# Sixteen expert slots repacked into thirteen, and the rank product of every block one step later

## The chip, the cores and the metric

The kernel runs on one core of a Trainium2 chip. The metric is the device time of one execution in microseconds (us); of several runs the median counts. Engines are named as in the profile: PE is TensorE (its matmuls; PEld its loading of the stationary operand), DVE VectorE, ACT ScalarE, POOL GpSimd, SP SyncE.

## The reference

Three stages on 3072 tokens of 384 features (4 batches of 768, 8 heads of 48): a linear recurrence, a dense MLP with a leaky ReLU, and a layer of 8 experts of which each token uses the one with the highest score.

```python
for t in range(S):                                   # 768 steps
    cur = einsum('bhd,bhe->bhde', u * k[t], v[t])
    y[t] = einsum('bhd,bhde->bhe', r[t], state + cur)
    state = w[t][..., None] * state + einsum('bhd,bhe->bhde', k[t], v[t])
x = y.transpose(0, 2, 1, 3).reshape(3072, 384)
h = x @ w_in                                         # 384 -> 2048
x = (maximum(h, 0) + alpha * minimum(h, 0)) @ w_out  # 2048 -> 384
logits = normalized(x) @ normalized(expert_emb).T / tau
e = argmax(logits); gate = softmax(logits)[e]
out[e == i] = gate * (maximum(x[e == i] @ w1[i], 0) @ w2[i])   # 384 -> 1024 -> 384
```

With the reference's inputs the eight experts get 193, 578, 253, 951, 286, 327, 365 and 119 tokens.

## The kernel before

**Precision.** Every operand of a large product is split into a high part (fp32r) and the rest, and a product is three matmuls: high x high, high x low, low x high. Names that end in h and l are these parts.

**Stages.** The recurrence is computed in 24 tiles (n) of 128 tokens, in chunked form, while the MLP runs: MLP blocks j = 0 to 7 take three tiles (384 tokens) each, in 16 steps of 128 hidden features. In a step T, TensorE does nine matmuls of 384 columns for the first layer (L453) and nine of 392 for the second one of two steps earlier (L488; its 8 columns beyond 384 are the routing scores). Parts of the recurrence of later tiles stand between steps: transposes kt_ps (L341), a_ps (L352), u_ps (L368), y_ps (L391, L394) and t_ps (L409), which turns the result y (written by DVE at L400) into the input of the next block.

**Routing.** `route(j)` is a Python generator that is advanced once in every step. It computes for block j the one-hot matrix `oh` of the chosen experts on DVE (L550), yields as often as HOLD says (`HOLD[0]` for blocks 0 to 5, `HOLD[1]` and `HOLD[2]` for blocks 6 and 7), and then forms the rank product rk_ps on PE (L564 to L567): how many tokens ahead went to the same expert. DVE turns it into positions s_ps (L569, L570), and in the next step s_pf and s_pi (L573, L575). SP then writes the token rows (L580), and POOL scatters the token numbers to the table `tbl` by position (L583).

**PSUM.** rk_ps, kt_ps, the two a_ps, u_ps, t_ps and x_ps are tiles of one pool of three banks and take turns in them; the h tiles have two banks, the o tiles three.

**Expert slots.** After the MLP come the slots, whose kinds stand in the string KIND. A pair slot (P) takes 256 rows of one expert in eight steps, each with nine matmuls of 256 columns (l3, L796) and, two steps later, six of 384 (l4, L822). A single slot (S) takes 128 rows in two steps: nine matmuls of 512 columns each (l3_single, L832), four transposes (L843) and twelve matmuls of 384 (l4_single, L854). The first ES slots are early: a small table after block 6 gives each an expert that has 256 rows by then. The others come from the late table (`last_table`, after block 7), which DVE computes while the early slots run. `columns` finds for each late slot its expert and its first row, by comparing all slots with the running sums of slots per expert (`le`), and writes idsx (rows, L649, L652) and wix (weights, L655). What does not fit runs in an extra pass (`tile_extra`).

**Around a slot.** Its weights come in four loads (L754, POOL's indirect DMA), and eight pieces are split into high (ACT, L765) and low (DVE, L766) in the steps from four before the slot's first to three behind it. Its rows are gathered (L777) and transposed (x_T: PE L785, ACT L786, DVE L787). Between l3 and l4, ACT and DVE make the hidden values g2h (L800) and g2l (L801). At the end ACT scales each o by the gate (L859), and POOL scatters the rows to the output (L861).

Of the kernel before, what the change touches and what calls it, by code (L numbers as in the profile page):

```python
# [8 lines left out]
F32 = mybir.dt.float32  # L9
# [9 lines left out]
DM = H * D  # L19
# [26 lines left out]
ES = 5  # L46
NP = 6
NS1 = 5
NPX = 3
C_P = ES  # L50
C_S = ES + NP + NPX
NSLOT = C_S + NS1
KIND = "PPPPP" + "SPSPSPPSPSP"
COL = [s if s < ES else C_P + KIND[ES:s].count("P") if k == "P" else C_S + KIND[:s].count("S") for s, k in enumerate(KIND)]
# [6 lines left out]
HOLD = [1, 2, 2]  # L61
# [45 lines left out]
def tile_main(ctx, tc, keep, x2d, tbl, att, w_in, w_out, alpha, u_row, u_col, emb, tau, w1, w2, cst, out):  # L107
# [20 lines left out]
    u_sb = cp.tile([128, DM], F32, name="u_sb")  # L128
# [167 lines left out]
    def att_u(n):  # L296
        r_n, k_n = nat(n, 0), nat(n, 1)
        POOL.tensor_tensor(out=r_n, in0=r_n, in1=k_n, op=ALU.mult)
        POOL.tensor_tensor(out=r_n, in0=r_n, in1=u_sb, op=ALU.mult)
# [326 lines left out]
    def columns(c0, n, at, cu, step, base, odd):  # L626
# [5 lines left out]
        ei = once("ei", [128, NSLOT])[:, 0:m]  # L632
# [3 lines left out]
        jb = once("jb", [128, NSLOT])[:, 0:m]  # L636
# [12 lines left out]
        DVE.tensor_scalar(out=idsx[:, c0:c0 + n], in0=jb[:, 0:n], scalar1=prow, scalar2=None, op0=ALU.add)  # L649
        yield  # L650
        if m > n:
            DVE.tensor_scalar(out=idsx[:, c0 + n:c0 + m], in0=jb[:, n:m], scalar1=2.0, scalar2=prow, op0=ALU.mult, op1=ALU.add)  # L652
        DVE.tensor_scalar(out=ei, in0=ei, scalar1=float(NE - 1), scalar2=256.0, op0=ALU.min, op1=ALU.mult)
        for q in range(2):
            DVE.tensor_scalar(out=wix[:, q, c0:c0 + m], in0=ei, scalar1=prow2, scalar2=float(q), op0=ALU.add, op1=ALU.add)  # L655

    def early_table():

        yield WAIT
        tot = totals(NB - 2, oneb[:, 0:1])  # L660
        nb = above(tot, thr_full, "nb")
        cu = once("cu", [128, 2 * NE])[:, 0:NE]
# [3 lines left out]
        yield from columns(0, ES, at_early, cu, nb, None, None)  # L666
# [21 lines left out]
    def last_table():  # L688
# [42 lines left out]
        yield from columns(C_P, NP + NPX, at_last, cu, n, first[:, 0:1], o)  # L731
# [38 lines left out]
    def ids_load(s):  # L770
        t = sp.tile([128, 2], I32, tag="ids", name="ids", bufs=5)
        n = NTOK[s]
        POOL.indirect_dma_start(out=t[:, 0:n], out_offset=None, in_=tbl.rearrange("(n t) o -> n (t o)", t=n), in_offset=idx(idsx[:, COL[s]:COL[s] + 1]))
        ids_t[s] = t

    def gather(s, t):
        POOL.indirect_dma_start(out=xg[s % 3][:, t, :], out_offset=None, in_=x2d, in_offset=idx(ids_t[s][:, t:t + 1]), bounds_check=NT - 1, oob_is_err=False)  # L777

    def x_T(s, t):
        if t == 0:  # L780
            xT2[s] = [xp.tile([128, KD, SLOT], F32R, tag=f"x{i}", name=f"y{i}") for i in "hl"]
        hi, lo = (x[:, :, t * 128:(t + 1) * 128] for x in xT2[s])
        tp = ps_a.tile([128, KD, 128], F32, tag="a", name="x_ps")
        for k in range(KD):
            PE.transpose(tp[:, k, :], xg[s % 3][:, t, k * 128:(k + 1) * 128], ident)  # L785
        ACT.activation(out=hi, in_=tp, func=AF.Copy)  # L786
        DVE.tensor_tensor(out=lo, in0=tp, in1=hi.bitcast(F32), op=ALU.subtract)  # L787

    def l3(s, f):
# [8 lines left out]
        gh = gp.tile([128, SLOT], F32R, tag="gh", name="g2h")  # L798
        gl = gp.tile([128, SLOT], F32R, tag="gl", name="g2l")
# [68 lines left out]
    if True:  # L868
        for l in LOADS:
            if l == "e":  # L870
                SP.dma_start(out=en, in_=emb)
            elif l == "u":
                SP.dma_start(out=u_sb, in_=u_row.to_broadcast([128, DM]))
# [19 lines left out]
        POOL.memset(carry[0], 0.0)  # L893
        POOL.iota(ivals, pattern=[[0, BT], [1, NE]], base=0, channel_multiplier=0, allow_small_or_imprecise_dtypes=True)
# [187 lines left out]
        for s, k in enumerate(KIND):  # L1082
            U0, before = FIRST[s], KIND[s - 1]
            at(U0 + (9 if k == "P" else 3), o_scale, s)
            if k == "P":
# [11 lines left out]
            if s:  # L1097
                X = U0 - 4 if before == "P" else U0 - 2
# [248 lines left out]
def tile_kernel(ctx, tc, att, w_in, w_out, alpha, u_row, u_col, emb, tau, w1, w2, cst, r, k, v, w, uh, out):  # L1347
# [8 lines left out]
    wix = kp.tile([128, 2, NSLOT], I32, name="wix")  # L1356
# [68 lines left out]
```

## Time and profile before

| | |
|---|---|
| Median of three runs | 805.92 us (805.19 to 807.06) |
| Profiled execution | 808.39 us |
| Its span, first to last instruction | 806.6 us |
| Mean granted clock of TensorE | 0.994 |
| Busy: PE, DVE, ACT, POOL | 98%, 71%, 55%, 38% of the span |
| Moved by DMA | 114.85 MB, 142 GB/s over the span |

The profiled execution is one run of its own, and the rows below belong to it. A timeline row has the start and the duration of an instruction or of a group of alike ones, its engine and line, what it writes and reads, and, in brackets, how long the engine had been idle before it and what ended that. Matmuls overlap: the pitch from one start to the next is what each costs in a stream, and it is less than a duration.

### The profile page before, as it was taken

Reading aid. Unit: us, or ns where it says so; the run is one execution under the profiler, and the core shown is the slowest. Engines: PE = TensorE matmul, PEld = TensorE weight load, DVE = VectorE, ACT = ScalarE, POOL = GpSimd, SP = SyncE. Lnnn points to the kernel's source line nnn. Section 1 sums busy time; section 2 is a strip of 40 time slices with the busy share of each in tenths; the row PEclk is TensorE's granted clock in tenths of the full one; section 3 lists DMA queues with packets and bytes.
Section 4 is the critical chain, followed back from the end, with each engine's and each line's share of the span. In section 5 each row is a group of like instructions: output and inputs, shape, how many; then the busy total and the mean of one; then the engine's idle time right before and its main releaser. Section 6 shows DMA issues by size and latency. Waiting matters only on the chain. (4 is left out here: it accounts for less than half of the span.)

```text
span 806.6 us, 16527 instructions
## 1 busy us (share of the span) xinstructions
PE 791.2 (98%) x6507; PEld 755.1 (94%) x6507; DVE 570.7 (71%) x1167; ACT 440.5 (55%) x885; POOL 303.5 (38%) x365
## 2 busy tenths in 40 slices
PE   9999999999999999999999999999999999999996
PEld 5789999899999999999999999999999999999996
DVE  8989867776666676666776763666996866767662
ACT  6887744445435435444533543446555776766762
POOL 3101122242242242133214212155456777777731
PEclk9999999999999999999999999999999999999999
DMA  9654411145335321123122100077697677776740
GB/s 321 227 187 160 149 70 62 42 86 188 99 75 167 126 47 69 68 93 69 70 100 69 69 32 1 30 160 252 206 200 239 226 248 287 260 261 223 271 151 33
DMA packets 31622, 114.85 MB, mean 142 GB/s; under 512 B 5756, under 2 KB 13148, under 8 KB 29232
## 3 DMA queue, kind: packets, MB, share of 16 engines
q0 software_dynamic: 13952, 59.86, 23.3%
q1 hardware_dynamic: 17584, 53.85, 21.0%
q8 instruction: 53, 0.87, 0.5%
q14 instruction: 33, 0.27, 0.1%
HBM read 99.36 MB, written 15.51 MB: 142 GB/s over the span
## 5 line engine op out<-in xcount | busy, mean ns | idle before, releaser
L463 ACT ACTIVATE m<-h_ps,al_sb 128x384 f32<-128x384 f32 x128 | 74.2, 581 | 140.1 <-PE h_ps L453 134.0
L467 DVE TENSOR_TENSOR m<-h_ps,m 128x384 f32<-128x384 f32 x128 | 70.8, 553 | 98.6 <-ACT m L463 97.3
L473 ACT ACTIVATE gh<-m 128x384 fp32r<-128x384 f32 x128 | 67.2, 525 | 107.5 <-DVE m L467 106.8
L478 DVE TENSOR_TENSOR gl<-m,gh 128x384 fp32r<-128x384 f32 x128 | 79.3, 620 | 36.3 <-ACT gh L473 36.1
L360 POOL TENSOR_SCALAR_AFFINE_SELECT A<-A 128x512 f32<-128x512 f32 x48 | 33.0, 711 | 185.4 <-ACT A L359 185.3
L754 POOL DMA_INDIRECT raw<-in_w,wix x64 | 67.6, 1056 | 55.5 <-DVE w0l L766 29.5
L796 PE MATMUL h_ps<-yh,w0h 128*128 128x256 f32 x264 | 76.5, 290 | 0.0
L796 PE MATMUL h_ps<-yl,w0h 128*128 128x256 f32 x264 | 74.5, 282 | 0.0
L766 DVE TENSOR_TENSOR w1l<-raw,w1h 128x768 fp32r<-128x768 f32 x64 | 60.6, 953 | 19.3 <-ACT w1h L765 18.6
L796 PE MATMUL h_ps<-yh,w0l 128*128 128x256 f32 x264 | 74.3, 281 | 0.0
L766 DVE TENSOR_TENSOR w0l<-raw,w0h 128x768 fp32r<-128x768 f32 x64 | 60.8, 957 | 12.1 <-ACT w0h L765 12.1
L453 PE MATMUL h_ps<-xh,win0h 128*128 128x384 f32 x192 | 68.8, 358 | 0.0
L453 PE MATMUL h_ps<-xh,win1h 128*128 128x384 f32 x192 | 68.2, 355 | 0.0
L309 POOL TENSOR_TENSOR sbd<-st,PS 48x192 f32<-48x192 f32 x40 | 27.3, 682 | 104.9 <-DVE PS L279 63.2
L488 PE MATMUL o_ps<-wout1h,gh 128*128 128x392 f32 x192 | 65.8, 343 | 0.0
L488 PE MATMUL o_ps<-wout0h,gh 128*128 128x392 f32 x192 | 65.8, 342 | 0.0
L488 PE MATMUL o_ps<-wout0h,gl 128*128 128x392 f32 x192 | 65.5, 341 | 0.3 <-DVE gl L478 0.3
L453 PE MATMUL h_ps<-xl,win0h 128*128 128x384 f32 x192 | 65.4, 341 | 0.0
L488 PE MATMUL o_ps<-wout0l,gh 128*128 128x392 f32 x192 | 65.4, 340 | 0.0
L488 PE MATMUL o_ps<-wout1h,gl 128*128 128x392 f32 x192 | 65.4, 340 | 0.0
L453 PE MATMUL h_ps<-xh,win0l 128*128 128x384 f32 x192 | 65.2, 340 | 0.0
L488 PE MATMUL o_ps<-wout1l,gh 128*128 128x392 f32 x192 | 65.2, 340 | 0.0
(284 smaller groups left out, 2301.8 us busy)
## 6 DMA issues: line engine op xcount, KB each, us to landing
ld<-in_att SPq DMA_DIRECT2D x18, 1348.5 KB, 6.8
stg<-in_w_in SPq DMA_DIRECT2D x24, 256.0 KB, 4.7
stg<-in_w_out SPq DMA_DIRECT2D x8, 768.0 KB, 6.9
x2d<-rows SPq DMA_DIRECT2D x24, 194.0 KB, 2.4
out<-zero SPq DMA_DIRECT2D x24, 192.0 KB, 6.6
ld<-in_att SPq DMA_DIRECT2D x5, 512.0 KB, 5.1
ld<-in_att SPq DMA_DIRECT2D x3, 452.5 KB, 5.2
raw<-in_w,wix POOLq DMA_INDIRECT x64, 6.1
```

The costliest lines, as they stand in the source:

```text
L309: POOL.tensor_tensor(out=s[q, :, D * i:D * i + D], in0=st[b][q], in1=R[q, :, 0:1].to_broadcast([D, HP, D]), op=ALU.mult)
L360: POOL.affine_select(out=h, in_=h, pattern=[[0, HP], [1, CH]], compare_op=ALU.is_gt, fill=0.0, base=0, channel_multiplier=-1)
L453: PE.matmul(out=h, lhsT=w[:, k, :], rhs=x[:, k, :], start=(n == 0), stop=(n == 3 * KD - 1))
L463: ACT.activation(out=m, in_=h_t[j, f], func=AF.Copy, scale=al_sb[:, f:f + 1])
L467: DVE.tensor_tensor(out=m, in0=h_t.pop((j, f)), in1=m, op=ALU.min)
L473: ACT.activation(out=gh, in_=m_t[j, f], func=AF.Copy)
L478: DVE.tensor_tensor(out=gl, in0=m_t.pop((j, f)), in1=gh.bitcast(F32), op=ALU.subtract)
L488: PE.matmul(out=o_t[j][i], lhsT=g[:, s], rhs=w, start=(f == 0 and n == 0), stop=(f == KF - 1 and n == 2))
L754: POOL.indirect_dma_start(out=t, out_offset=None, in_=src, in_offset=idx(wix[:, h, COL[s]:COL[s] + 1]))
L766: DVE.tensor_tensor(out=lo, in0=a, in1=hi.bitcast(F32), op=ALU.subtract)
L796: PE.matmul(out=h, lhsT=w[:, k, :], rhs=x[:, k, :], start=(n == 0), stop=(n == 3 * KD - 1))
```

## The change

**Slots.** KIND goes from 11 P and 5 S (five P early) to 8 P, 2 S and 3 of a new kind T (four P early, then TSPTSPTPP). A T slot takes a pair of an expert and its remainder of at most 72 rows: 328 rows in eight steps of nine matmuls of 328 columns and nine of 384, the last three with 72 stationary columns. Its third piece of rows has its own list (`idsx` columns from C_T on) and is gathered to u_sb, which the recurrence no longer needs by then. It takes three o banks. The late table finds up to three experts with a pair to be placed late and a remainder of at most 72 (`el`), takes these out of the pairs and the singles, and puts them ahead. NPX goes from 3 to 7 slots of the extra pass, so `columns` works on 16 late slots and 24 running sums where it had 14 and 16.

**HOLD** goes from [1, 2, 2] to [2, 2, 2].

```diff
-ES = 5
-NP = 6
-NS1 = 5
-NPX = 3
+ES = 4
+NT1 = 3
+TL = 72
+NP = NT1 + 4
+NS1 = 2
+NPX = 7
...
-KIND = "PPPPP" + "SPSPSPPSPSP"
+KIND = "PPPP" + "TSPTSPTPP"
...
-STEPS = [(s, i) for s, k in enumerate(KIND) for i in range(8 if k == "P" else 2)]
-NTOK = [2 if k == "P" else 1 for k in KIND]
+STEPS = [(s, i) for s, k in enumerate(KIND) for i in range(2 if k == "S" else 8)]
+NTOK = [{"P": 2, "T": 3, "S": 1}[k] for k in KIND]
+ROWS = [CH, CH, TL]
...
-HOLD = [1, 2, 2]
+HOLD = [2, 2, 2]
...
-            hi = once("hi", [128, NSLOT])[:, 0:m]
-            DVE.tensor_scalar(out=hi, in0=ei, scalar1=float(NE), scalar2=-float(NE), op0=ALU.is_ge, op1=ALU.mult)
+            hi = once("hi", [128, NP + NPX + NS1])[:, 0:m]
+            DVE.tensor_scalar(out=hi, in0=ei, scalar1=2.0 * NE, scalar2=-float(NE), op0=ALU.is_ge, op1=ALU.mult)
+            DVE.tensor_tensor(out=hi, in0=ei, in1=hi, op=ALU.add)
+            DVE.tensor_scalar(out=ei, in0=ei, scalar1=float(NE), scalar2=-float(NE), op0=ALU.is_ge, op1=ALU.mult)
...
+        DVE.scalar_tensor_tensor(out=over, in0=pr, scalar=-float(SLOT), in1=tot[:, 0:NE, 0], op0=ALU.mult, op1=ALU.add)
+        DVE.tensor_tensor(out=rest, in0=pr, in1=done, op=ALU.subtract)
+        DVE.scalar_tensor_tensor(out=over, in0=over, scalar=float(TL), in1=odd, op0=ALU.is_le, op1=ALU.mult)
+        yield
+        DVE.scalar_tensor_tensor(out=over, in0=rest, scalar=1.0, in1=over, op0=ALU.is_ge, op1=ALU.mult)
+        DVE.tensor_tensor_scan(el, over, over, 0.0, ALU.add, ALU.bypass)
+        DVE.scalar_tensor_tensor(out=el, in0=el, scalar=float(NT1), in1=over, op0=ALU.is_le, op1=ALU.mult)
+        DVE.tensor_tensor(out=rest, in0=rest, in1=el, op=ALU.subtract)
+        DVE.tensor_tensor(out=odd, in0=odd, in1=el, op=ALU.subtract)
+        yield
...
+        if NTOK[s] == 3:
+            c = C_T + KIND[:s].count("T")
+            POOL.indirect_dma_start(out=t[0:TL, 2:3], out_offset=None, in_=tbl, in_offset=idx(idsx[0:TL, c:c + 1]))
...
+    def rows_of(s, t):
+        return u_sb[0:TL] if t == 2 else xg[s % 3][:, t]
...
-        h = ps_h.tile([128, SLOT], F32, tag="h", name="h2_ps")
+        h = ps_h.tile([128, width(s)], F32, tag="h", name="h2_ps")
...
-            o2_t[s] = [ps_o.tile([128, DM], F32, tag="o", name="o2_ps") for _ in range(2)]
+            o2_t[s] = [ps_o.tile([128, DM], F32, tag="o", name="o2_ps") for _ in range(NTOK[s])]
...
-                PE.matmul(out=o2_t[s][t], lhsT=g[:, c], rhs=w, start=(f == 0 and n == 0), stop=(f == KE - 1 and n == 2))
+                PE.matmul(out=o2_t[s][t][0:ROWS[t]], lhsT=g[:, c], rhs=w, start=(f == 0 and n == 0), stop=(f == KE - 1 and n == 2))
```

HOLD moves instructions in all of blocks 0 to 5. In block 0, on PE, from the last second-layer matmul of a step to the recurrence of the tile, before (lines are those of each kernel, and four higher in the new one; s_oh is `oh`, trib and oneb are constants, carry the counts of the blocks ahead):

```order
L488 MATMUL o_ps<-wout0h,gl 128x392
L564 LDWEIGHTS trib
L564 MATMUL rk_ps<-s_oh,trib 128x24
L566 LDWEIGHTS oneb
L566 MATMUL rk_ps<-s_oh,oneb 128x16
L566 LDWEIGHTS oneb
L566 MATMUL rk_ps<-s_oh,oneb 128x8
L567 LDWEIGHTS oneb
L567 MATMUL rk_ps<-carry_118,oneb 128x24
L368 MATMUL u_ps<-ld,Kt 48x48 x8
```

And at the end of the next step in the same block, on PE, after:

```order
L492 MATMUL o_ps<-wout1h,gl 128x392
L568 LDWEIGHTS trib
L568 MATMUL rk_ps<-s_oh,trib 128x24
L570 LDWEIGHTS oneb
L570 MATMUL rk_ps<-s_oh,oneb 128x16
L570 LDWEIGHTS oneb
L570 MATMUL rk_ps<-s_oh,oneb 128x8
L571 LDWEIGHTS oneb
L571 MATMUL rk_ps<-carry_118,oneb 128x24
L413 MATMUL t_ps<-ident,y 128x128 x3
```

The four matmuls of the rank product have moved from ahead of u_ps to ahead of t_ps.

In block 2, on PE, at the end of the step ahead of kt_ps, before:

```order
L488 MATMUL o_ps<-wout1l,gh 128x392
L488 MATMUL o_ps<-wout1h,gl 128x392
L341 MATMUL kt_ps<-ident,ld 128x128 x4
L352 MATMUL a_ps<-ld 128x128 x8
L453 MATMUL h_ps<-xh,win1h 128x384
```

The same place after:

```order
L492 MATMUL o_ps<-wout1h,gl 128x392
L568 LDWEIGHTS trib
L568 MATMUL rk_ps<-s_oh,trib 128x24
L570 LDWEIGHTS oneb
L570 MATMUL rk_ps<-s_oh,oneb 128x16
L570 LDWEIGHTS oneb
L570 MATMUL rk_ps<-s_oh,oneb 128x8
L571 LDWEIGHTS oneb
L571 MATMUL rk_ps<-carry_118,oneb 128x24
L345 MATMUL kt_ps<-ident,ld 128x128 x4
L356 MATMUL a_ps<-ld 128x128 x8
L457 MATMUL h_ps<-xh,win1h 128x384
```

The rank product, which stood one step ahead, is now directly ahead of kt_ps and a_ps, the next tiles of its pool.

On DVE in block 2, around the two instructions that read rk_ps (L569 and L570), before:

```order
L335 TENSOR_TENSOR dv<-ld,dg 128x384
L478 TENSOR_TENSOR gl<-m,gh 128x384
L569 TENSOR_TENSOR s_ps<-rk_ps,ebase 128x24
L570 TENSOR_TENSOR s_ps<-s_ps,s_oh 128x24
L467 TENSOR_TENSOR m<-h_ps,m 128x384
```

And after (L573 and L574 there):

```order
L339 TENSOR_TENSOR dv<-ld,dg 128x384
L482 TENSOR_TENSOR gl<-m,gh 128x384
L471 TENSOR_TENSOR m<-h_ps,m 128x384
L482 TENSOR_TENSOR gl<-m,gh 128x384
L573 TENSOR_TENSOR s_ps<-rk_ps,ebase 128x24
L574 TENSOR_TENSOR s_ps<-s_ps,s_oh 128x24
```

The two have moved behind the m and gl of the following step.

## Rows read from the trace of the kernel before

**Rows 1.** The page, first part: busy time, share of the span, instructions.

```profile
PE 791.2 (98%) x6507; PEld 755.1 (94%) x6507; DVE 570.7 (71%) x1167; ACT 440.5 (55%) x885; POOL 303.5 (38%) x365
```

**Rows 2.** Waits of PE: for what, us in total, times, longest.

```profile
PE rk_ps L564 <- DVE s_oh L550: 1.9, 1, 1.9
...
PE x_ps L785 <- DMA xg<-x2d,ids: 0.6, 2, 0.3
```

**Rows 3.** Timeline of PE in a pair slot: start, duration, engine, line, operands.

```profile
576.37 0.28 PE L796 MATMUL h_ps<-yh,w0h 128*128 128x256 f32 x1
...
577.44 0.33 PE L822 MATMUL o_ps<-w1h,g2h 128*128 128x384 f32 x1
...
578.49 0.28 PE L796 MATMUL h_ps<-yh,w0h 128*128 128x256 f32 x1
```

**Rows 4.** Timeline of PE in a single slot and the slot behind it.

```profile
643.41 0.39 PE L832 MATMUL h_ps<-w0h,yh 128*128 128x512 f32 x1
...
645.50 0.34 PE L822 MATMUL o_ps<-w1h,g2h 128*128 128x384 f32 x1
...
648.98 0.60 PE L843 MATMUL g_ps<-ident,Kt 128*128 128x128 f32 x4
649.33 0.42 PE L822 MATMUL o_ps<-w1h,g2h 128*128 128x384 f32 x1
649.59 0.34 PE L822 MATMUL o_ps<-w1l,g2h 128*128 128x384 f32 x1
```

**Rows 5.** Timeline of PE in block 0, at the rank product.

```profile
154.29 0.19 PE L564 MATMUL rk_ps<-s_oh,trib 128*128 128x24 bf16 x1 [1.92 <-DVE s_oh L550]
...
154.48 0.88 PE L368 MATMUL u_ps<-ld,Kt 128*48 128x48 f32 x16
...
158.10 0.44 PE L453 MATMUL h_ps<-xh,win1h 128*128 128x384 f32 x1
...
161.39 0.49 PE L409 MATMUL t_ps<-ident,y 128*128 128x128 f32 x3
```

**Rows 6.** Stretch 154 to 158: busy PE, PEld, DVE, ACT, POOL, clock, DMA.

```profile
154.00:158.00 4.00, 3.71 (x68) 3.68 (x68) 3.81 (x14) 0.52 (x1) 0.00 (x0) 0.57 0.01 4
```

**Rows 7.** Timeline of PE, the same part of a later tile.

```profile
173.11 0.56 PE L368 MATMUL u_ps<-ld,Kt 128*48 128x48 f32 x16
...
175.19 0.44 PE L453 MATMUL h_ps<-xh,win1h 128*128 128x384 f32 x1
```

**Rows 8.** Timeline of DVE in block 0.

```profile
157.41 0.72 DVE L376 TENSOR_TENSOR st<-u_ps,sbd 48x192 f32<-48x192 f32 x2
158.22 0.56 DVE L400 TENSOR_TENSOR y<-y_ps,dv 128x384 f32<-128x384 f32 x1
```

**Rows 9.** Timeline of PE in block 2.

```profile
290.68 1.16 PE L352 MATMUL a_ps<-ld 64*128 64x128 f32 x16
```

**Rows 10.** Timeline of DVE in block 2.

```profile
289.68 0.18 DVE L569 TENSOR_TENSOR s_ps<-rk_ps,ebase 128x24 f32<-128x24 f32 x1
...
289.99 0.55 DVE L467 TENSOR_TENSOR m<-h_ps,m 128x384 f32<-128x384 f32 x1
291.13 0.56 DVE L478 TENSOR_TENSOR gl<-m,gh 128x384 fp32r<-128x384 f32 x1 [0.59 <-ACT gh L473]
```

**Rows 11.** DVE while the table is computed: a row of its timeline, a stretch.

```profile
588.33 0.38 DVE L631 TENSOR_TENSOR le<-s_cu,at_last 128x224 f32<-128x224 f32 x1
...
588.00:594.00 6.00, 6.00 (x44) 6.00 (x43) 5.83 (x16) 2.87 (x6) 3.89 (x4) 1.00 0.84 86
```

**Rows 12.** End of the table (DVE), slot 4's weights (POOL, ACT; loads on the page).

```profile
596.79 0.37 DVE L655 TENSOR_SCALAR wix<-s_ei,prow 128x14 int32<-128x14 f32 x2
...
598.15 1.06 POOL L754 DMA_INDIRECT raw<-in_w,wix  x1 [0.31 <-issue]
...
618.47 0.84 ACT L765 ACTIVATE w0h<-raw 128x768 fp32r<-128x768 f32 x1
...
raw<-in_w,wix POOLq DMA_INDIRECT x64, 6.1
```

More of the change, by code (lines that the diff above doesn't have):

```diff
@@ L298, in att_u @@
         POOL.tensor_tensor(out=r_n, in0=r_n, in1=k_n, op=ALU.mult)
-        POOL.tensor_tensor(out=r_n, in0=r_n, in1=u_sb, op=ALU.mult)
+        POOL.tensor_tensor(out=r_n, in0=r_n, in1=u_sb[:, 0:DM], op=ALU.mult)
     def att_6D(n):
@@ L624, in above, with columns @@
         return nb
-    def columns(c0, n, at, cu, step, base, odd):
+    def columns(c0, n, at, cu, step, base, odd, none):
         m, k = at.shape[1], cu.shape[1]
@@ L665, in early_table @@
         yield
-        yield from columns(0, ES, at_early, cu, nb, None, None)
+        yield from columns(0, ES, at_early, cu, nb, None, None, None)
         yield
@@ L703, in last_table @@
-        DVE.tensor_scalar(out=first[:, NE:2 * NE], in0=b, scalar1=-1.0, scalar2=None, op0=ALU.add)
-        DVE.scalar_tensor_tensor(out=n, in0=n, scalar=2.0, in1=first[:, 0:2 * NE], op0=ALU.mult, op1=ALU.add)
+        n = once("v", [128, BT, NE]).rearrange("p i e -> p (i e)")
+        el, rest, odd = (n[:, NE * i:NE * (i + 1)] for i in range(3))
+        over = once("ex", [128, BT, NE])[:, 0, :]
+        DVE.scalar_tensor_tensor(out=odd, in0=pr, scalar=-2.0, in1=b, op0=ALU.mult, op1=ALU.add)
+        DVE.scalar_tensor_tensor(out=over, in0=pr, scalar=-float(SLOT), in1=tot[:, 0:NE, 0], op0=ALU.mult, op1=ALU.add)
@@ new lines, in last_table @@
+        DVE.tensor_tensor(out=odd, in0=odd, in1=el, op=ALU.subtract)
+        yield
+        cu = once("lg", [128, BT, NE]).rearrange("p i e -> p (i e)")
+        DVE.tensor_tensor_scan(cu, n, n, 0.0, ALU.add, ALU.bypass)
+        first = once("first", [128, 3 * NE + 1])
+        DVE.memset(first, 0.0)
+        DVE.tensor_scalar(out=first[:, 0:NE], in0=pr, scalar1=2.0, scalar2=-2.0, op0=ALU.mult, op1=ALU.add)
+        DVE.tensor_scalar(out=first[:, NE:2 * NE], in0=done, scalar1=2.0, scalar2=None, op0=ALU.mult)
@@ L705, in last_table @@
+        DVE.tensor_scalar(out=first[:, 2 * NE:3 * NE], in0=b, scalar1=-1.0, scalar2=None, op0=ALU.add)
+        yield
+        DVE.scalar_tensor_tensor(out=n, in0=n, scalar=2.0, in1=first[:, 0:3 * NE], op0=ALU.mult, op1=ALU.add)
         DVE.tensor_tensor(out=n, in0=n, in1=first[:, 1:], op=ALU.subtract)
-        tp, ts = cu[:, NE - 1:NE], cu[:, 2 * NE - 1:2 * NE]
-        yield
+        tt, tp, ts = (cu[:, i * NE - 1:i * NE] for i in range(1, 4))
+        none = once("none", [128, NT1])
+        DVE.tensor_scalar(out=none, in0=ip[:, 0:NT1], scalar1=tt, scalar2=float(NE * NT), op0=ALU.is_ge, op1=ALU.mult)
@@ L730, in last_table @@
         yield
-        yield from columns(C_P, NP + NPX, at_last, cu, n, first[:, 0:1], o)
+        yield from columns(C_P, NP + NPX, at_last, cu, n, first[:, 0:1], o, none)
         yield DONE_T
@@ L804, in l4_last @@
     def l4_last(s, fs):
-        for t in range(2):
+        for t in range(NTOK[s]):
             for f in fs:
@@ L810, in l4_last, with l4 @@
             del g2_t[s, f]
-    def l4(s, f, ts=(0, 1)):
+    def l4(s, f, ts=None):
         gh, gl = g2_t[s, f]
-        if ts == (0, 1):
+        if ts is None:
+            ts = range(NTOK[s])
             del g2_t[s, f]
@@ L857, in o_scale @@
         for t in range(NTOK[s]):
-            o = sp.tile([128, DM], F32, tag=("y", "dv")[t], name="o2")
-            ACT.activation(out=o, in_=o2_t[s][t], func=AF.Copy, scale=xg[s % 3][:, t, DM:DM + 1])
+            p = slice(0, ROWS[t])
+            o = sp.tile([128, DM], F32, tag=("y", "dv", "y")[t], name="o2")
+            ACT.activation(out=o[p], in_=o2_t[s][t][p], func=AF.Copy, scale=rows_of(s, t)[p, DM:DM + 1])
             POOL.memset(spin, 0.0)
-            ins = POOL.indirect_dma_start(out=out, out_offset=idx(ids_t[s][:, t:t + 1]), in_=o, in_offset=None, bounds_check=NT - 1, oob_is_err=False)
+            ins = POOL.indirect_dma_start(out=out, out_offset=idx(ids_t[s][p, t:t + 1]), in_=o[p], in_offset=None, bounds_check=NT - 1, oob_is_err=False)
             if s or t:
@@ L1090, in tile_main @@
                     at(U0 + i, relu_single, s, i)
-            if s and before == "P":
-                for n, i in enumerate((4, 5, 6, 7) if k == "P" else (2, 3, 4, 5, 5, 6, 6, 7)):
+            if s and before != "S":
+                for n, i in enumerate((4, 5, 6, 7) if k != "S" else (2, 3, 4, 5, 5, 6, 6, 7)):
                     at(U0 - 8 + i, split, s, n)
@@ L1109, in l34 @@
                 s, i = STEPS[U - lag]
-                fn = pair if KIND[s] == "P" else single
+                fn = single if KIND[s] == "S" else pair
                 if fn:
```

56 lines of the change are left out of this document (28 added, 28 removed).

## The prediction

> **What bounds the kernel now.** I read the page first. TensorE is busy for 791.2 of the 806.6 us span [rows 1], so time can go in two ways only: fewer or narrower matmuls, or one of TensorE's few waits. The view of its waits has two that matter here: 1.9 us once, the rank product L564 waiting for the one-hot `oh` of DVE, and 0.6 us in two pieces at L785, where gathered token rows had not landed [rows 2]. The change touches both kinds: the expert slots alter the matmuls, HOLD alters where L564 stands.
>
> Next the pitch of matmuls, from one start to the next, since their durations overlap. In a pair slot nine matmuls of 256 columns (L796) take 577.44 - 576.37 = 1.07 us, 0.119 each, and six of 384 columns (L822) take 1.05, 0.175 each; a step is 2.12 us and a pair slot (8 steps) 17.0 us [rows 3]. In a single slot nine of 512 columns (L832) take 2.09 us, 0.232 each; a group of transposes (L843) takes 0.35, and the matmul behind it 0.26 for 0.175, so 0.09 more [rows 4].
>
> **Part 1: columns.** Before, expert rows fill 11 pair slots and 5 single ones. The reference's inputs give the experts 193, 578, 253, 951, 286, 327, 365 and 119 rows: 11 pairs, and remainders of 66, 30, 71, 109 and 119 rows. Three are at most 72 and belong to an expert with a pair, so after, 3 slots of 328 rows, 8 pairs and 2 singles hold everything exactly. Three times, a pair and a single become one slot of 328.
>
> A single slot: 18 x 0.232 + 24 x 0.175 + 2 x (0.35 + 0.09) = 9.3 us. With its pair: 26.3. A slot of 328: 72 matmuls of 328 columns and 72 of 384 (for the third piece only the stationary side is narrower, and L822's pitch goes by moving columns). No row has 328 columns. Below and above stand 0.119 (256) and 0.175 (384); 512 gives 0.232, so 128 columns cost 0.056 or 0.057 over the whole stretch, a straight line, and I take 0.119 + 72/128 x 0.056 = 0.151. The slot is 72 x 0.151 + 72 x 0.175 = 23.5 us, and the saving 2.75 x 3 = **8.2 us**. If 328 columns were charged as 384 the slot would be 25.2, the saving 1.1 x 3 = 3.2; if as 256, 21.2 and 15.3. The straight line through three widths makes both ends unlikely. Tiles to transpose stay 27 in number (L785). All of this lies on TensorE, which nothing covers: it counts in full.
>
> The pitches here are 0.119 and 0.232 us for 256 and 512 columns, each matmul with a weight load of its own [rows 3, 4]. The Trainium skill, "TensorE: Matmul & The Clock Gate", section "Back-to-back issue gap", gives about 81 ns for 128 columns and 131 ns for 512 in such a stream. An estimate by that page: 0.098, 0.107 and 0.114 for 256, 328 and 384, and a saving of about 7 us rather than 8.2. The rows are well above the page's prices, so the measured pitches decide.
>
> **Part 2: the rank product a step later.** In block 0 TensorE stops 1.92 us for `oh`, until 154.29; then L368 to L394 take 154.48 to 158.10 = 3.62 us, and t_ps starts at 161.39 [rows 5]. The granted clock is 0.57 in 154 to 158, that is largely the 1.2 GHz level behind the pause [rows 6]; the same instructions take 2.08 us elsewhere [rows 7]. After, L368 goes straight on at 152.37: 2.08 brings the next L453 to 154.45, its step (161.39 - 158.10 = 3.29) ends at 157.74, and the rank product there adds the 0.19 that it takes now (154.29 to 154.48), `oh` being long done. That would put t_ps at 157.93, a gain of 3.5. But t_ps needs y of DVE (L400), which ends at 158.22 + 0.56 = 158.78, behind L376 at 157.41 [rows 8]; DVE is not faster for the change, except that the two rank instructions (0.31 us for the same pair in block 2, 289.68 to 289.99 in [rows 10]) no longer stand ahead of L376. So y is done at 158.47, t_ps starts about 158.54, and the gain is **2.85** (ends 0 and 3.5). A pause of some 0.7 us is left at t_ps.
>
> Blocks 1 to 5 had no such wait [rows 2], so nothing is gained there. In blocks 1 to 3 something can be lost. The rank product now stands directly ahead of kt_ps and the two a_ps (L341, L352), and these four tiles share three PSUM banks: the second a_ps needs the bank of rk_ps, free once DVE has done L569. Before, that was read at 289.68, and a_ps started at 290.68 without waiting [rows 9, 10]. After, L569 stands behind the step's next m and gl. Those need no rank product: m moves from 289.99 to 289.68, gl from 291.13 to 290.82 [rows 10], it holds DVE some 0.5 and L569 0.18, which ends at about 291.5. a_ps would have started at 290.68 + 0.19 = 290.87: **0.65 us of new wait, three times, 2.0 us**. Bounds: 0 (if the scheduling of banks differs) and 0.9 each. Nothing is added for the clock: it fell behind a pause of 1.92 us, three times as long. Blocks 4 and 5 have no kt_ps at that step. What moves along, POOL's scatter of the block's positions and SP's row writes, goes one step (3.3 us) later, and is read only after the last block: nothing.
>
> **Part 3: a longer table.** The late table is computed on DVE during the early slots. There DVE is busy 5.83 of 6 us [rows 11] with the splits of weights, the g2l of every step and table work between them. The change adds about 12 small instructions (0.18 each, as L569 in [rows 10]) and makes four products of `columns` 128x384 for 128x224: 0.55 (m in [rows 10]) for 0.38 [rows 11]. That is 2.2 + 0.7 = 2.9 us, plus one step of waiting. Where it piles up g2l comes later and TensorE can wait for an L796 bank; step by step I get up to 1 us. TensorE already loses 0.6 us at two gathers right behind that [rows 2], which would have landed meanwhile, so I take **+0.2**, bounds -0.3 and +2.
>
> The table ends at 596.79 + 0.37 before and some 3 us later after. Slot 4 is the first that needs it: its first load is issued at 598.15, a load lands after 6.1 us (median), and its first split is at 618.47 [rows 12]: 14 us of cover, of which 3 go. If that were gone, each us would be one on TensorE.
>
> **Part 4: free or nearly.** 12 fewer loads, 24 fewer splits on ACT and on DVE: off the path, 0. A slot of 328 holds all three o banks, so the next slot's first L822 waits until ACT has scaled the first of them; nine L796 (1.07 us) lie between and cover it: 0, and I allow 0.5 at each of five changes of slot for the case that they don't.
>
> **Sum:** -8.2 - 2.85 + 2.0 + 0.2 = -8.85 us. The profiled execution, 808.39 us (span 806.6), would become 799.5; it lies 2.5 us above the median of the runs, 805.92, so the forecast on that scale is **797.1 us**.
>
> **The rivals.**
> A. The rank product is free: banks or DVE's order spare the second a_ps, and block 0 gives up to 3.5. Then -8.2 - 2.85 (or -3.5) + 0.2: 794.4 to 795.1. For it: a_ps's wait is argued from an order, not seen. Against: L569 stands behind gl in three blocks.
> B. DVE binds in the early slots: its 2.9 us more come out on TensorE, with 0.5 us at several changes of slot: +2 to +5 over the sum, 799 to 802. For: 5.83 of 6 us busy. Against: the two waits already there absorb the first part.
> C. Width is not a straight line: 328 columns charged as 384, saving 3.2 rather than 8.2: 802.2. Against: three widths on one line.
> D. Slower: the rows do not fit. Expert 5's remainder is 71 of 72 rows. Two rows more there (near-ties decided otherwise than in the reference) and it needs a third single slot, of which there are two; its rows then run in the extra pass after the last slot (tile_extra), which goes through all 24 tiles with 24 matmuls of 128 columns and 8 of 384 each. At pitches on the line (0.063 and 0.175) that is 24 x 2.9 = 70 us at least, with nothing to hide it: 867 or more. It decides from 73 rows on. Against: the counts leave the row of margin.
> E. The change of slots saves, but the late table makes slot 4 wait over 8 us, and nothing is left: about 806. That takes a table 20 us late, against 3 reckoned.
>
> **How the numbers follow.** The sum as forecast, within 1.2 us: 0.52. A 0.15, B 0.19, C 0.03, D 0.04, E 0.04; 0.03 is left for a slowdown that I don't see. 0.2% is 1.6 us, about what a measurement of this kernel can tell from no change. Faster: the forecast, A, B and C, 0.89. Same: E, 0.04. Slower: D and the rest, 0.07. The range takes in the forecast, A and the nearer half of B: 794.4 to 800.6, with 0.8 of the chance.
>
> **What would show it.** Right: three stretches of nine matmuls with 328 columns at 0.151, 1.36 us each; slots of 328 at 23.5 us; no wait at L564 in block 0, t_ps near 158.5 and the clock at 1.00 there; waits of 0.65 us at a_ps behind DVE's ps in blocks 1 to 3. Wrong: a pitch of 0.175 at 328 columns (C); L796 or its weight splits waiting on DVE between 580 and 605 beyond 1 us (B); work behind the last slot (D); no wait at a_ps (A).

## The result and the profile after

The changed kernel takes 796.96 us (median of four runs, 794.69 to 798.12); the kernel before, beside it, 805.56 (803.25 to 807.06). The ratio is 0.9892, with a 95% interval of 0.986 to 0.9925: 8.6 us less. The forecast was 797.1. The profiled execution took 798.12 us with a span of 796.3, 10.3 less than the span before, so a part of that difference is not the change's; the section on why accounts for it.

Busy time of TensorE on the page of the kernel after [rows 1 has it before]: it fell by 10.5 us, as much as the span, so TensorE is as full as it was.

```profile
PE 780.7 (98%) x6429; PEld 744.4 (93%) x6429; DVE 554.6 (70%) x1150; ACT 418.4 (53%) x849; POOL 276.1 (35%) x354
```

The waits of PE after (for what: us in total, times, longest). The rank product's 1.9 us and the gathered rows' 0.6 us [rows 2] are gone. In their place stand three waits of a_ps for s_ps, one more at t_ps, and 0.3 us for g2l. Two waits at the start of the program, for Kt and for A, are 0.2 and 0.4 us longer than before.

```profile
PE a_ps L356 <- DVE s_ps L573: 1.2, 3, 0.4
PE t_ps L413 <- DVE y L404: 1.1, 2, 0.6
...
PE h_ps L826 <- DVE g2l L831: 0.3, 1, 0.3
```

A step in a slot of 328 rows, timeline of PE (start, duration, engine, line, operands). Nine matmuls from 632.25 to 633.61 are 0.151 each; nine of 384 columns from 633.61 to 635.20 are 0.177 each, and the last three, with 72 stationary columns, are no shorter. The step is 2.95 us for 2.12 [rows 3].

```profile
632.25 0.31 PE L826 MATMUL h_ps<-yh,w0h 128*128 128x328 f32 x1
...
633.61 0.34 PE L853 MATMUL o_ps<-w1h,g2h 128*128 128x384 f32 x1
...
634.67 0.34 PE L853 MATMUL o_ps<-w1h,g2h 128*72 128x384 f32 x1
634.84 0.34 PE L853 MATMUL o_ps<-w1l,g2h 128*72 128x384 f32 x1
...
635.20 0.31 PE L826 MATMUL h_ps<-yh,w0h 128*128 128x328 f32 x1
```

Block 0 on PE after: no wait ahead of u_ps, the stretch from 151.34 to 153.43 is 2.09 us for 3.62 [rows 5], and t_ps waits 0.51 us for y.

```profile
151.34 0.56 PE L372 MATMUL u_ps<-ld,Kt 128*48 128x48 f32 x16
...
153.43 0.45 PE L457 MATMUL h_ps<-xh,win1h 128*128 128x384 f32 x1
...
156.73 0.19 PE L568 MATMUL rk_ps<-s_oh,trib 128*128 128x24 bf16 x1
...
157.50 0.55 PE L413 MATMUL t_ps<-ident,y 128*128 128x128 f32 x3 [0.51 <-DVE y L404]
```

DVE there, and the stretch 154 to 158 (busy time of PE, PEld, DVE, ACT, POOL, then the granted clock: 1.00 for 0.57 in [rows 6]). The two instructions on rk_ps are no longer ahead of L380.

```profile
156.14 0.72 DVE L380 TENSOR_TENSOR st<-u_ps,sbd 48x192 f32<-48x192 f32 x2
156.88 0.56 DVE L404 TENSOR_TENSOR y<-y_ps,dv 128x384 f32<-128x384 f32 x1
...
154.00:158.00 4.00, 3.49 (x25) 3.23 (x24) 3.95 (x9) 1.17 (x3) 0.00 (x0) 1.00 0.87 248
```

Block 2 after, PE and then DVE. The first two a_ps matmuls start at 287.60, the others at 288.49, when s_ps has been read; before, all sixteen ran through from 290.68 [rows 9], with s_ps long done [rows 10].

```profile
287.04 0.64 PE L345 MATMUL kt_ps<-ident,ld 128*128 128x128 f32 x4
287.60 0.49 PE L356 MATMUL a_ps<-ld 64*128 64x128 f32 x2
288.49 1.16 PE L356 MATMUL a_ps<-ld 64*128 64x128 f32 x14 [0.40 <-DVE s_ps L573]
289.57 0.44 PE L457 MATMUL h_ps<-xh,win1h 128*128 128x384 f32 x1
...
287.78 0.56 DVE L482 TENSOR_TENSOR gl<-m,gh 128x384 fp32r<-128x384 f32 x1 [0.59 <-ACT gh L477]
288.25 0.18 DVE L573 TENSOR_TENSOR s_ps<-rk_ps,ebase 128x24 f32<-128x24 f32 x1
```

The table stretch after, DVE and then PE. A product of `columns` is 0.55 us for 0.38 [rows 11]; TensorE waits 0.30 once for g2l, and at 599.55 and 602.00 the gathered rows are there.

```profile
588.73 0.55 DVE L635 TENSOR_TENSOR le<-s_lg,at_last 128x384 f32<-128x384 f32 x1
...
598.34 0.37 DVE L663 TENSOR_SCALAR wix<-s_ei,prow 128x16 int32<-128x16 f32 x2
...
595.20 0.39 PE L826 MATMUL h_ps<-yh,w0h 128*128 128x256 f32 x1 [0.30 <-DVE g2l L831]
599.55 0.49 PE L812 MATMUL x_ps<-ident,xg 128*128 128x128 f32 x3
602.00 0.49 PE L812 MATMUL x_ps<-ident,xg 128*128 128x128 f32 x3
```

Slot 4's first load (POOL) and first split (ACT) are 17 us apart. The load lands after 5.5 us (median), so some 12 us of cover are left, for 14 [rows 12].

```profile
599.38 1.38 POOL L774 DMA_INDIRECT raw<-in_w,wix  x1 [2.47 <-ACT g2h L830]
...
616.65 0.84 ACT L785 ACTIVATE w0h<-raw 128x768 fp32r<-128x768 f32 x1
```

### The profile page after: what moved, and what is told of

It reads as the page before. It is cut to its first block, busy times and chain, and to the rows that moved or that the text cites. A ratio compares the mean times of both kernels' runs of the same rounds, so it can differ in the third digit from the quotient of the medians.

```text
span 796.3 us, 16277 instructions
## 1 busy us (share of the span) xinstructions
PE 780.7 (98%) x6429; PEld 744.4 (93%) x6429; DVE 554.6 (70%) x1150; ACT 418.4 (53%) x849; POOL 276.1 (35%) x354
## 3 DMA queue, kind: packets, MB, share of 16 engines
q1 hardware_dynamic: 17584, 53.85, 21.1%
q0 software_dynamic: 12128, 50.42, 20.8%
## 4 chain that ended last, share of the span: by engine, by line
PE 82%; DVE 7%; DMA 4%; issue 3%; ACT 3%; SPq 1%; POOL 0%; POOLq 0%; DVEq 0%; ACTq 0%
PE h_ps L457 24%; PE o_ps L492 23%; PE o_ps L853 11%; PE h_ps L826 11%; PE a_ps L356 3%; PE y_ps L398 2%; PE y_ps L395 2%; DMA stg<-in_w_in 1%; PE o_ps L885 1%; PE h_ps L863 1%; PE x_ps L812 1%; PE u_ps L372 1%; PE t_ps L413 1%; DMA stg<-in_w_out 1%; DVE m L471 1%
## 5 line engine op out<-in xcount | busy, mean ns | idle before, releaser
L826 PE MATMUL h_ps<-yh,w0h 128*128 128x256 f32 (+1 forms) x264 | 79.3, 301 | 0.3 <-DVE g2l L831 0.3
L774 POOL DMA_INDIRECT raw<-in_w,wix x52 | 55.5, 1066 | 64.5 <-DVE w0l L786 31.4
L826 PE MATMUL h_ps<-yl,w0h 128*128 128x256 f32 (+1 forms) x264 | 76.7, 291 | 0.0
L826 PE MATMUL h_ps<-yh,w0l 128*128 128x256 f32 (+1 forms) x264 | 76.6, 290 | 0.0
L830 ACT ACTIVATE g2h<-h_ps 128x256 fp32r<-128x256 f32 (+1 forms) x88 | 35.3, 401 | 72.9 <-PE h_ps L826 72.7
L853 PE MATMUL o_ps<-w1l,g2h 128*128 128x384 f32 (+1 forms) x200 | 67.6, 338 | 0.0
L853 PE MATMUL o_ps<-w1h,g2h 128*128 128x384 f32 (+1 forms) x200 | 67.6, 338 | 0.0
L853 PE MATMUL o_ps<-w1h,g2l 128*128 128x384 f32 (+1 forms) x200 | 67.6, 338 | 0.0
L457 PE MATMUL h_ps<-xh,win1l 128*128 128x384 f32 x192 | 64.9, 338 | 0.0
```

Source lines behind the costliest of these rows:

```text
L457: PE.matmul(out=h, lhsT=w[:, k, :], rhs=x[:, k, :], start=(n == 0), stop=(n == 3 * KD - 1))
L774: POOL.indirect_dma_start(out=t, out_offset=None, in_=src, in_offset=idx(wix[:, h, COL[s]:COL[s] + 1]))
L826: PE.matmul(out=h, lhsT=w[:, k, :], rhs=x[:, k, :], start=(n == 0), stop=(n == 3 * KD - 1))
L830: ACT.activation(out=gh, in_=h, func=AF.Relu)
L853: PE.matmul(out=o2_t[s][t][0:ROWS[t]], lhsT=g[:, c], rhs=w, start=(f == 0 and n == 0), stop=(f == KE - 1 and n == 2))
```

## The experiments

Twelve experiments were run in three groups, each group on a chip of its own with the kernel before beside it. The medians of before were 811.05, 811.9 and 807.19 us there, and each kernel is compared with the one of its group. The ratios below are those on record with their intervals; they differ from the quotient of the medians by up to 0.002. On the chips of the first two groups single runs scatter by 10 us, so the main reading is the length of four stretches in each kernel's profile, from start to start of matmuls on PE's timeline:

- **B0**: block 0, from the first-layer step ahead of the pause (149.02 before) to the one behind t_ps (161.63): two steps.
- **B2**: block 2, the step with kt_ps (286.89 to 291.77 before); blocks 1 and 3 agree with it within 0.03.
- **early**: the first 30 expert steps (555.04 to 621.75 before).
- **late**: from there to the last matmul.

```
kernel                           group  ratio to before [95%]     B0     B2    early   late
before (first profile)             -    -                        12.61   4.88  66.71  177.26
changed (first profile)            -    0.9892 [0.986, 0.9925]    9.74   5.82  66.60  168.78
e1  old slots, HOLD [2,2,2]        1    1.0015 [0.999, 1.004]     9.74   5.84  68.41  177.25
e2  new slots, HOLD [1,2,2]        1    0.9882 [0.9849, 0.9914]  11.06   4.88  68.33  170.06
e3  new slots, block 0 alone       1    0.9848 [0.9815, 0.9881]   9.78   4.88  68.25  170.06
e4  changed, third piece of 128    1    0.9989 [0.9959, 1.0019]   9.76   5.83  69.31  176.94
e5  before again                   2    1.0    [0.9959, 1.0042]  12.62   4.88  69.95  177.29
e6  changed again                  2    0.9946 [0.9909, 0.9983]   9.76   5.84  69.68  169.92
e7  changed, behind a_ps           2    0.9893 [0.9845, 0.9941]   9.76   4.79  67.42  171.36
e8  changed, longer table          2    0.9963 [0.9924, 1.0002]   9.76   5.84  69.52  171.92
e9  old slots, block 0 alone       3    0.9977 [0.9963, 0.9992]   9.74   4.88  68.34  177.30
e10 changed again                  3    0.9884 [0.9865, 0.9904]   9.74   5.83  66.61  168.78
e11 new slots, block 0 alone       3    0.9858 [0.9837, 0.988]    9.75   4.88  66.61  168.78
e12 new slots, HOLD [1,2,2]        3    0.9875 [0.9853, 0.9896]  11.08   4.88  66.59  168.78
```

**e1: the later rank product alone.** The kernel before with

```diff
-HOLD = [1, 2, 2]
+HOLD = [2, 2, 2]
```

> The kernel before with the rank product a step later in blocks 0 to 5, slots as they were. Theory (block 0 gains 2.9 us since the pause at the rank product and the half clock behind it go; blocks 1 to 3 lose 0.86 each because the second a_ps waits for the bank that DVE's s_ps frees): from the first MLP step to the first expert step about 0.3 us less, a median within 1 us of the kernel before. In the trace t_ps of block 0 comes 2.9 us earlier than before and a_ps waits in three blocks. Rival 1: the wait at a_ps costs only the 0.4 us that the view of waits counts: 1.7 us less. Rival 2: the rank product carries much of the whole gain: 4 us less or more.

813.69 us for 811.05, ratio 1.0015: no gain. B0 is 9.74 for 12.61, and B2 and its two sisters grow from 4.88 to 5.84, as in the changed kernel with the new slots. Rivals 1 and 2 fall: by itself this half of the change is worth nothing that can be measured. The 4 us that this profile adds in *early* (1.7) and just ahead of it (2.3) have their like in e5, which has no edit (3.2 and 3.7, on the second chip), so nothing ties them to the edit.

**e2 and e12: the slots alone.** The changed kernel with HOLD = [1, 2, 2], on two chips.

> The changed kernel with the rank product where it was (one wait less in blocks 0 to 5). Theory: the slots alone bring 8.2 to 8.6 us, so 797.0 to 797.5 beside 805.6 before, and the 1.9 us wait at the rank product of block 0 is back. Rival: the slots bring much less alone (below 6 us), since part of the gain comes from the rank product.

> The changed kernel with the rank product where it stood before in all blocks, beside the two ahead. Theory: between them, 0 to 1.3 us less than the changed kernel and 1.3 to 2.9 more than the one with block 0 alone. Rival (the later rank product pays on the whole): over 1 us more than the changed kernel.

0.9882 and 0.9875: the slots alone bring as much as the whole change. The rival of e2 falls (its interval is 7.0 to 12.2 us less), and so does that of e12. In the third group e12 is 10.95 us below before, more than the 8.2 to 8.6 that were expected of the slots. Three things can be read in the profiles. *Late* falls by 8.48 us (177.26 to 168.78). *Early* falls where the old slots waited longer for gathered rows, as in e9 (68.34, for 66.59 here). And B0 is 11.06 and 11.08, not 12.61: the wait is there, but the clock isn't lost behind it. In e12 on PE, and the stretch 154 to 158:

```profile
152.32 0.19 PE L568 MATMUL rk_ps<-s_oh,trib 128*128 128x24 bf16 x1 [1.92 <-DVE s_oh L554]
...
152.51 0.56 PE L372 MATMUL u_ps<-ld,Kt 128*48 128x48 f32 x16
...
154.60 0.44 PE L457 MATMUL h_ps<-xh,win1h 128*128 128x384 f32 x1
...
154.00:158.00 4.00, 4.00 (x42) 3.91 (x39) 3.50 (x9) 1.00 (x3) 0.00 (x0) 1.00 0.56 166
```

The same pause of 1.92 us as in [rows 5], and 2.09 us for u_ps and y_ps instead of 3.62. So the later rank product takes 1.3 us out of block 0 here (11.08 to 9.75), not 2.85. Against e10, e12 is 0.7 us shorter. The intervals of the two overlap, but the stretches say the same: the later rank product costs 2.3 us in the blocks behind block 0 and gains 1.3 in it.

**e3 and e11: block 0 alone.** The changed kernel with

```diff
-HOLD = [2, 2, 2]
+HOLD = [2, 1, 1, 1, 1, 1, 2, 2]
...
-        for _ in range(HOLD[max(j - NB + 3, 0)]):
+        for _ in range(HOLD[j]):
```

> The changed kernel with the rank product a step later in block 0 alone; in blocks 1 to 5 it stands where it stood before. Theory (the new wait of a_ps costs 0.86 us in each of blocks 1 to 3): 2.6 us less than the changed kernel, about 794.4, no wait at a_ps left, block 0 as fast as in the changed kernel. Rival 1 (the wait costs what the view of waits counts, 0.4 each): 1.2 us less. Rival 2 (the wait is hidden by a later one): no difference.

> The changed kernel with the rank product a step later in block 0 alone, beside the one ahead. Theory: 2.6 us less than it, in blocks 1 to 3 alone (4.88 us for 5.85 in their step with kt_ps). Rival: within 0.8 us of it.

0.9848 and 0.9858. B0 keeps its 9.75, B2 is back at 4.88, no wait of a_ps is left. Beside the changed kernel in group 3 it takes 795.01 us for 796.97, 2.0 less, and no run of one reaches a run of the other; the ends of the two profiles differ by 2.3. Both are nearer to 2.6 than to the 1.2 that the view of waits adds up to. **This is the best version**: it has the lowest median of its group both times.

**e4: 384 columns for 328.** The changed kernel with

```diff
-TL = 72
+TL = 128
```

> The changed kernel with third pieces of up to 128 rows: its three large slots have 384 columns for 328, the same rows are computed. Theory (a matmul is charged by its columns on a straight line, 0.151 us for 328 and 0.1755 for 384): 72 x 0.0245 x 3 = 5.3 us more than the changed kernel, and no difference in the matmuls whose stationary side goes from 72 to 128 columns (0.175 both). Rival 1 (328 columns already pay as 384): no difference. Rival 2 (the stationary width is charged too): more than 5.3 us, by a longer pitch of the last 72 L853 matmuls of the slots.

811.13 us. Every step of the three large slots is 0.22 us longer than in the changed kernel (24 steps, 5.3 us), and nine matmuls take 641.12 to 642.70 = 1.58, 0.1755 each. The nine L853 behind take 1.59, as long as with 72 stationary columns (above). So the prices of 256, 328, 384 and 512 columns lie on one line, and 72 stationary columns cost here what 128 do: rivals 1 and 2 fall.

```profile
641.12 0.34 PE L826 MATMUL h_ps<-yh,w0h 128*128 128x384 f32 x1
...
642.70 0.34 PE L853 MATMUL o_ps<-w1h,g2h 128*128 128x384 f32 x1
...
644.29 0.49 PE L812 MATMUL x_ps<-ident,xg 128*128 128x128 f32 x3
```

*Late* grew by 6.9 us against e2 and e3 on that chip, 1.6 more than the steps explain. Of this 0.9 lies in single waits at the changes of slot (0.48, 0.48 and 0.67 us, for 0.20 and 0.53 in e2), such as e7 and e8 have without this edit; the rest was not traced.

**e5: the kernel before again.**

> The kernel before once more, beside the others of this group. Theory: the pause of 1.9 us at the rank product of block 0 is there again, but what it costs isn't fixed: where the granted clock falls behind it, the stretch from that step to the one two later lasts 12.6 us, where it doesn't, 11.1. Rival: the clock always falls there when the slots are the old ones, 12.6.

811.37 us for 811.9, and B0 is 12.62: with the old slots the clock fell behind the pause in both profiles that have it, with the new slots in neither (e2, e12). The rival as put down fits these four, but other pauses of the same profiles show that it isn't the slots. With the old ones the clock stayed at 1.00 behind a pause of 1.90 us ahead of the first expert step (e1). With the new ones it fell behind one of 1.42 us ahead of wt_ps near the start (e4), as it did there in the first profile of the kernel before, and it stayed behind one of 1.63 us there in the changed kernel:

```profile
48.24 1.37 PE L244 MATMUL wt_ps<-ident,stg 128*128 128x128 f32 x6 [1.42 <-ACT Kt L344]
49.26 0.67 PE L453 MATMUL h_ps<-xh,win0h 128*128 128x384 f32 x1
...
48.81 0.98 PE L248 MATMUL wt_ps<-ident,stg 128*128 128x128 f32 x6 [1.63 <-ACT Kt L348]
49.55 0.42 PE L457 MATMUL h_ps<-xh,win0h 128*128 128x384 f32 x1
```

The first two lines are before (granted clock 0.50 from 48.6 to 52.0), the others after (1.00). Nor need the clock fall in every run of the old kernel: in group 3 the three of its 17 runs with a mean granted clock of 0.998 took 804.3 to 804.8 us, the others, with 0.995 to 0.997, 805.3 to 809.1. What decides it is open.

**e6 and e10: the changed kernel again.**

> The changed kernel once more, beside the others of this group. Theory: in block 0 the stretch of two steps lasts 9.7 us as before, in blocks 1 to 3 the step with kt_ps lasts 5.83 to 5.85 us for 4.88, and the whole is 1.1 per cent below the kernel before. Rival: the gain was one of the first chip, and is below 0.5 per cent here.

> The changed kernel beside the next two on one chip. Theory: 8.2 us of the slots, 1.3 to 2.9 of block 0, less 2.6 in blocks 1 to 3: 0.989 of the kernel before. Rival: on a chip with slower loads the slots keep only about 6 us of theirs, 0.993.

0.9946 on the slower chip, 0.9884 on the other. The 1.1 per cent expected of e6 was missed: its interval ends at 0.9 per cent less, and the rival, a gain below 0.5 per cent, can't be told apart from the 0.54 measured. The stretches of blocks 0 to 3 repeat within 0.03 us on all three chips, so what differs lies elsewhere, for the most part in the expert stage. *Late* is 177.25 to 177.30 with the old slots on every chip. With the new ones it is 168.78 in the first profile and in group 3, 169.92 to 171.92 in groups 1 and 2 (e2, e3, e6, e7, e8): there the slots keep 5.3 to 7.3 of their 8.5 us. So the rival of e10 (about 6) names something real, but of those chips and not of e10's. Its reason, slower loads, is not borne out: the packets of POOL's queue took 21.0 to 21.3% of the span on those chips and 20.8 to 21.1% elsewhere. What stands in *late* there, and not in the first profile, e10, e11 or e12, is idle time of ACT ahead of g2h and of DVE ahead of g2l that nothing in the profile ends (7.6 and 3.8 us in e2). The old slots have some of it too (1.4 and 1.2 us in e1), without a cost in *late*.

**e7: behind a_ps in blocks 1 to 3.** The changed kernel with HOLD[j] as in e3 and

```diff
+HOLD = [2, 3, 3, 3, 1, 1, 2, 2]
```

> The changed kernel with the rank product two more steps later than at first in blocks 1 to 3 (behind kt_ps and a_ps, one step later than in the changed kernel), where it was in blocks 4 and 5. Theory (the wait of a_ps comes from sharing a bank with rk_ps, not from being late): no wait at a_ps, that step back from 5.85 to 4.9 us, 2.6 us less than the changed kernel. Rival (whatever stands a step later for DVE delays TensorE there): the wait moves to the next tile of that pool and costs as much, no difference.

No wait of a_ps, B2 4.79; the rank product follows a step later at 289.75 and nothing waits for it. PE in block 2 of e7:

```profile
285.37 1.16 PE L356 MATMUL a_ps<-ld 64*128 64x128 f32 x16
...
289.75 0.19 PE L568 MATMUL rk_ps<-s_oh,trib 128*128 128x24 bf16 x1
```

So it was the order within the shared banks, and not the later time as such. The medians, 802.89 for 807.11 of e6, go the same way; their distance is more than the edit's, since the chip's own pauses are in them. The longest of those in e7 is one wait ahead of the experts:

```profile
PE o_ps L492 <- ACT gh L477: 5.7, 1, 5.7
```

**e8: a longer table.** The changed kernel, in `columns` after each of the two reductions:

```diff
+        for _ in range(2 if base is not None else 0):
+            DVE.tensor_reduce(out=ei, in_=le, axis=AX.X, op=ALU.add)
...
+        for _ in range(2 if base is not None else 0):
+            DVE.tensor_reduce(out=jb, in_=le, axis=AX.X, op=ALU.add)
```

> The changed kernel with the two reductions of the late table made three times each: four more DVE instructions of 0.55 us, 2.2 us in all, same result. Theory (the longer table of the change was free only because it took the place of two waits for gathered rows, and these are used up): TensorE loses 1 to 2.2 us between the 15th and the 21st step of the early slots. Rival 1 (DVE has room there): below 0.3 us. Rival 2 (a late table holds up slot 4's weights as well): over 3 us.

809.59 us, 2.5 more than e6; by the medians alone this isn't clear of the scatter. In the profile, steps 16 to 18 are 2.5 us longer than in the changed kernel's first one, for 2.2 us of DVE work and a little above the 1 to 2.2 expected, and PE waits there for g2l:

```profile
596.41 0.39 PE L830 MATMUL h_ps<-yh,w0h 128*128 128x256 f32 x1 [1.04 <-DVE g2l L835]
599.84 0.39 PE L830 MATMUL h_ps<-yh,w0h 128*128 128x256 f32 x1 [1.03 <-DVE g2l L835]
```

Rival 1 falls. Slot 4 has no new wait on its weights, so rival 2 falls too: DVE is full there, and these 2.2 us of table work cost 2.5.

**e9: block 0 alone, old slots.** The kernel before with e3's edit.

> The kernel before with the rank product a step later in block 0 alone. Theory: no new wait, and the stretch of two steps in block 0 falls from 12.62 to 9.76 us where the clock fell before, from 11.06 where it didn't: 1.3 to 2.9 us less than the kernel before, so a ratio of 0.9965 to 0.9984. Rival (a later wait takes it back): below 0.5 us.

804.74 us for 807.19, ratio 0.9977 [0.9963, 0.9992]: 2.45 us less by the medians, 0.6 to 3.0 by the interval. B0, by itself, is 2.87 shorter than in the first profile; the rival falls. In this profile the old slots waited longer for gathered rows than in [rows 2]:

```profile
PE x_ps L785 <- DMA xg<-x2d,ids: 2.2, 2, 1.1
```

## Why the prediction was right, step by step

**Columns: right, 8.2 forecast, 8.5 measured.** The pitch at 328 columns is 0.151, the value on the straight line; the ends 3.2 and 15.3 are out (e4). The other part of the step, that all of it counts on TensorE, holds where no change of slot waits. The 0.3 us more is a term that was counted at nothing: the transposes of a 72-row piece take 0.15 us for 0.24, three times. On PE after:

```profile
622.13 0.35 PE L812 MATMUL x_ps<-ident,u_sb 72*128 72x72 f32 x3
622.28 0.36 PE L826 MATMUL h_ps<-yh,w0h 128*128 128x256 f32 x1
```

By an estimate from the prices of the Trainium skill ("TensorE: Matmul & The Clock Gate", "Back-to-back issue gap") for streams with a weight load each, the saving would have been about 7 us (7.7 with the single slots' transposes at the rows' 0.88). The rows had spoken against these prices, and the 0.151 us measured at 328 columns, for 0.107 by that estimate, bears the rows out.

**Block 0: right to 0.02 us in this pair of profiles, 2.87 for 2.85, but half of it is the clock's and not the pause's alone.** B0 went from 12.61 to 9.74, t_ps waits 0.51 us as the view counts and some 0.7 from start to start, as reckoned. The step took the fallen clock for a fixed part of the pause. e2 and e12 have the pause and keep the clock, and there the move is worth 1.3. With the old slots it is 2.87 beside the first profile and e5's, and 2.45 in the runs of e9. What decides whether the clock falls behind a pause of 1.92 us was not found: the pause is as long, TensorE was full ahead of it in both, and the place in the program is the same. The kind of slots is not what decides (e5).

**Blocks 1 to 3: the mechanism was right, the term too small.** 0.65 us each was forecast; the step grew by 0.96, of which 0.12 is the rank product itself, moved in from the step ahead, so 0.84. The error is in the start that a_ps would have had: 0.19 was added to it for the rank product, though this had left the step ahead of it and TensorE came as early as before. 0.65 + 0.19 = 0.84. In blocks 4 and 5 the step that the rank product has left is 0.11 shorter and the next one no longer. From block 1 to the first expert step the profiles of e10 and e12 differ by 2.26 us (395.55 for 393.29), where 2.0 stood in the sum.

**Table: right that it is hidden, at about zero for +0.2.** Steps 18 to 20 became 0.8 us longer, the two with gathered rows behind them 0.95 shorter; *early* is 66.60 for 66.71. wix came 45.0 us behind the first expert step for 41.75: 3.25 us later, forecast 3. e8 shows that no more than this was free. In other profiles of the old slots the rows came later still (*early* 68.34 in e9, for 66.6 of the new slots beside it), so against those the change gains up to 1.7 us there.

**Free parts: right on two chips.** No change of slot waits in the changed kernel's first profile, in e10, e11 or e12. On the chips of groups 1 and 2 the new slots lose 1.1 to 3.1 us in *late*, the old ones nothing. The 0.5 at five changes of slot had been allowed for, but for another reason: the waits are not at the o banks but ahead of first-layer matmuls, for yl, yh, w1l or g2l where the profile names what ended them (0.2 to 1.2 us each). Why the new slots are hit and the old ones are not is not shown; less slack around fewer and larger slots is a guess.

**The profile's 10.3 us.** From the last matmul's start, 799.01 to 788.71: -0.96 ahead of block 0, -2.87 in it, +2.12 in blocks 1 to 7, -0.11 in *early*, -8.48 in *late*. The first is the clock too: in the profile of before it fell at 48.6, and that MLP step took 2.91 us for 1.66 after, 1.25 more (lines above); the rest is a start 0.29 us later after. The old kernel did that stretch in 147.18 in e9 and 146.75 in e5, for 149.02 in the first profile, and that step in 1.66 and 1.67, so this isn't the change's. Without it 9.3 remain, for 8.85 forecast. So that the median came within 0.2 us of the forecast is luck in part: columns and table brought 0.3 us each more than forecast, blocks 1 to 5 0.3 less, and block 0 is worth 1.3 to 2.9 from run to run.

**The rivals.** A, no wait at a_ps: out. B, DVE: its extra work was felt (0.8 us) and paid for by the gathers. C, width: out. D, an extra pass: nothing stands behind the last slot. E: out, slot 4's cover was 12 us.

The medians agree with the sums: e10 is 10.2 us below before (0.9865 to 0.9904 of 807.19 is 7.7 to 10.9 less), where the stretches give 2.87 + 8.48 + 0.1 to 1.7 - 2.3, so 9.2 to 10.8 (1.5 less where the clock stays up behind the pause).

## What to carry to other kernels

Where TensorE is full, a change of width is worth the number of matmuls times the difference in their pitch, and the pitch of a width that no row has could be read here off a line through the widths on both sides of it. A step moved out of one wait can make the next tile of its buffer pool wait: look at who gets the bank next, in every block in which the order differs, and move only the blocks that waited. A fallen clock behind a wait is not part of the wait's fixed price: take it out of the sum, or put it in the range. Added work on a full engine is free only as long as it takes the place of another wait; find out how much of that wait is left.

## What had not been expected of the hardware

- A pause of 1.92 us on TensorE cost its clock in two profiles (0.57 over the next 4 us in the first, largely the 1.2 GHz level, then 1.00) and left it at 2.4 GHz in two others, with 1.5 us of difference in what followed. One of 1.42 us cost it too, and ones of 1.63 and 1.90 us didn't. The price of a pause in one profile may not hold in the next run.
- The view of waits gave 0.40 us for the wait of a_ps; the starts give 0.89 from one a_ps group to the next, and the step is 0.84 us longer. The view counts from the modelled end of the two matmuls ahead (0.49 us after the start of the first), and in a stream this tail is time in which others start: all sixteen start within 1.1 us in e7.
- On two of the chips single pauses of 0.3 to 6 us stood in ACT's or DVE's stream around the first expert steps, and smaller ones in the slots, in old and new kernels alike (TensorE waits 5.7 us for ACT in e7). The profile names no engine of the core as what ends most of ACT's, and their cause stays open.
